# Attention on one core: the states of two heads multiplied as dense 64x64 blocks on quarters of the array

## The chip, the core and the metric

The kernel runs on one core of a Trainium2 chip. The metric is the device time of one execution in microseconds, lower is better. TensorE multiplies matrices into PSUM, which has eight banks of 2 KB in each of 128 partitions; VectorE (DVE), ScalarE (ACT) and GpSimd (POOL) do elementwise work, and DMA queues are fed by SyncE (SP) and GpSimd.

## The reference

```python
B, H, S, D = 8, 8, 576, 64          # q, k, v: batch, heads, sequence, head size
scores = q @ k.T / sqrt(D)
gamma = 1 - 2 ** (-5 - h)           # one decay for each head h
ret = scores * (gamma ** (i - j) if i >= j else 0)
attn = ret @ v                       # retention: no softmax
x = attn as (B*S, H*D) = (4608, 512)
x = moe1(x)    # cosine routing to one of 8 experts, 512 -> 1024 -> 512, relu, times the gate
x = moe2(x)    # greedy routing with a capacity of 576 tokens an expert, same sizes
```

Only the first part, attention, is touched by the change. With decay by distance, the part of a row's output that comes from earlier tiles can be written as q times a state of 64x64 for each head, the sum of gamma ** (-j) * k_j times v_j over earlier rows j, with gamma ** i put into q.

## The kernel before

The 4608 rows are 36 tiles of 128, nine tiles to two sequences of 576 rows: tile i = 0 to 3 lies in the first sequence, tile 4 holds the last 64 rows of the first and the first 64 of the second, tiles 5 to 8 lie in the second. So tile 0 of each nine has no state before it, tile 4 has one for 64 of its columns, and the other seven for all 128. Everything is float32. q and k arrive transposed, as tiles of 128 partitions (64 dimensions of the even head, then 64 of the odd one) x 4 head pairs x 128 rows; v and k also arrive by rows.

The order of the instructions is written out by hand: each engine runs them in the order of the program. The loop over T in the function moe_kernel does in iteration T, in this order: the loads of tile T + 3 (load_tile, on SP's queue, four buffers each); s_qk(T + 1); s_sel(T - 2); s_pv(T); a step of the routing of an earlier group of tiles (pump, route); s_state(T); s_kd(T + 2) on GpSimd; s_out(T - 1); s_qs(T + 2) on VectorE. The pieces are:

- s_qk, line 402: scores of the tile's diagonal block, for each head pair hp and each head e of the pair one product with 64 rows of the array, into the tiles s0 and s1, one PSUM bank each. VectorE multiplies them by the decay (line 405) into sm.
- s_sel, line 473: a small product that puts the router's logits together. Its input part is copied by ScalarE in line 461.
- s_pv: the output of the tile, transposed, in one PSUM bank o. First, where there is a state, line 416: for each head pair one product of 128x128, in which bd holds the states of the two heads as two 64x64 blocks on the diagonal, with zeros beside them; qs is q times its decay. Then line 420: for each head the product of v and sm, on 64 columns of the array, added on top. ScalarE copies o to xT (line 423).
- s_state, line 438: adds the tile's product of kd (k times its decay, made by GpSimd in line 379) and v to the state, which stays in one PSUM bank st over four tiles; ScalarE copies the two diagonal blocks to bd (line 444), in two instructions of 64x256. The zeros beside the blocks are written once, at the start (line 337), by a memset on VectorE and one on GpSimd.
- s_out: the product of xT with the expert embedding (line 458, on 32 columns of the array for each pair) and four transposes of xT (line 464) into tp, which has two buffers of one bank; ScalarE copies tp to xg (line 465).

PSUM is full: s0, s1, o, st, two banks for logits, two for tp. The routed rows are scattered to DRAM by GpSimd (line 534), group by group. In the last tiles the loads of the first expert's rows and weights begin on SP's queue (lines 311 and 241), the weights from T = 31 on, and from T = 32 on ScalarE and GpSimd or VectorE split each weight into a high and a low part (lines 267 and 272). Then come two expert stages, to which the change does nothing.

Of the kernel before, what the change touches and what calls it, by code (L numbers as in the profile page):

```python
# [9 lines left out]
F32 = mybir.dt.float32  # L10
# [3 lines left out]
AF = mybir.ActivationFunctionType  # L14
# [5 lines left out]
B, H, S, D = 8, 8, 576, 64  # L20
N, DM, E, FF = 4608, 512, 8, 1024
NT = N // 128
# [16 lines left out]
LOG2E = 1.4426950408889634  # L39


def constants():
    g = 1.0 - 2.0 ** (-5.0 - np.arange(H, dtype=np.float64))
    p = np.arange(128)
    rel = p[None, :] - p[:, None]
    dt = np.where(rel[:, None, :] >= 0, g[None, :, None] ** np.maximum(rel, 0)[:, None, :], 0.0) / 8.0
    s = np.arange(64, 192)
    gq, gs = np.empty((128, 4, 128)), np.empty((128, 4, 3))
    for e in range(2):
        for hp in range(4):  # L50
            gq[64 * e:64 * e + 64, hp, :] = (g[2 * hp + e] ** s / 8.0)[None]
            gs[64 * e:64 * e + 64, hp, :] = (g[2 * hp + e] ** np.array([128.0, 256.0, 384.0]))[None]
    tl = np.arange(9)[None, :, None]
    pos = 128 * tl + p[:, None, None]
    pos = np.where(pos >= S, pos - S, pos)
    gk = g[None, None, :] ** (-pos.astype(np.float64))
    sel = np.zeros((128, E))
    for q in range(4):
        for e in range(E):
            sel[32 * q + e, e] = 1.0  # L60
    tri = (p[:, None] < p[None, :]).astype(np.float64)
    f = np.float32
    blk = {}
    for nj in (32, 4, 2):
        r = np.arange(4 * nj)
        m = np.zeros((4 * nj, 4, E))
        m[r, r // nj, :] = 1.0
        blk[f"c_blk{nj}"] = m.reshape(4 * nj, 4 * E).astype(np.float32)
        blk[f"c_rep{nj}"] = (r[:, None] % nj == np.arange(nj)[None, :]).astype(np.float32)
    r = np.arange(8)  # L70
    blk["c_rz"] = np.repeat(np.stack([r % 2 == 0, r % 2 == 1], 1).astype(np.float32), 128, 1)
    s16 = np.zeros((16, E), np.float32)
    s16[np.arange(16), np.arange(16) % E] = 1.0
    return {
        **blk, "c_s16": s16,
        "c_dt": np.ascontiguousarray(dt.reshape(128, 4, 2, 128).transpose(0, 2, 1, 3)).astype(f), "c_gq": gq.astype(f), "c_gs": gs.astype(f),
        "c_gk": gk.reshape(128, 72).astype(f), "c_sel": sel.astype(f),
        "c_id": np.eye(128, dtype=f), "c_tri": tri.astype(f),
    }
# [78 lines left out]
def moe_kernel(ctx: ExitStack, tc: tile.TileContext, moe_expert_emb, moe_tau, moe_w1, moe_w2,  # L158
               moe2_w_gate, moe2_w1, moe2_w2, c, out, dbg=None, stage=9):
    nc = tc.nc  # L160
    V, A, G, P, SY = nc.vector, nc.scalar, nc.gpsimd, nc.tensor, nc.sync
# [151 lines left out]
    with tc.tile_pool(name="actab", bufs=1) as tab, \  # L313
# [17 lines left out]
        dt_t = tab.tile([128, 2, 4, 128], F32, name="dt")  # L331
        SY.dma_start(dt_t, c["c_dt"])
        load_tile(0, ("vr", "kr"))
        bd = []
        for i in range(2):
            t = tab.tile([128, 4, 128], F32, name=f"bd{i}")
            (G if i else V).memset(t, 0.0)
            bd.append(t)
        taub = tab.tile([128, 1], F32, name="taub")
        SY.dma_start(taub, ap(moe_tau, 0, [[0, 128], [1, 1]]))  # L340
        emb = tab.tile([E, DM], F32, name="emb")
# [20 lines left out]
        st_ps = [None]  # L362
# [45 lines left out]
        def s_pv(T):  # L408
            i = T % 9
            nq = nq_of(i)  # L410
            vt, sm = TL[T]["vr"], SM.pop(T)
            op_ = ps.tile([128, 4, 128], F32, name="o")
            if nq:
                qs, bdl = QS.pop(T), BD.pop(T)
                for hp in range(4):
                    P.matmul(op_[:, hp, :nq], bdl[:, hp, :], qs[:, hp, :nq], start=(hp == 0), stop=False,
                             skip_group_check=True)
            for hp in range(4):
                for e in range(2):
                    P.matmul(op_[64 * e:64 * e + 64, hp, :], vt[:, 2 * hp + e, :], sm[:, e, hp, :],  # L420
                             start=(hp == 0 and not nq), stop=True, skip_group_check=True)
            xT = wk.tile([128, 4, 128], F32, name="xT")
            A.activation(xT, op_, AF.Copy)  # L423
            XTT[T] = xT

        def s_state(T):
            i = T % 9
            t = TL.pop(T)
            if i == 8:
                return  # L430
            vt = t["vr"]
            r0 = 64 if i == 4 else 0
            kd = KDT.pop(T)
            if i in (0, 4):
                st_ps[0] = ps.tile([128, 4, 128], F32, name="st")
            for hp in range(4):
                for e in range(2):
                    P.matmul(st_ps[0][64 * e:64 * e + 64, hp, 64 * e:64 * e + 64], kd[r0:, 2 * hp + e, :],  # L438
                             vt[r0:, 2 * hp + e, :], start=(i in (0, 4) and hp == 0), stop=(i in (3, 7)),
                             skip_group_check=True)  # L440
            nb = bd[i % 2]
            for e in range(2):
                z = slice(64 * e, 64 * e + 64)
                A.activation(nb[z, :, z], st_ps[0][z, :, z], AF.Copy)
            BD[T + 1] = nb

        def s_out(T):
# [11 lines left out]
                         skip_group_check=True)  # L459
            part = wk.tile([128, 128], F32, name="part")  # L460
            A.activation(part, lp[:, :128], AF.Copy)
            xp = ps.tile([128, 4, 128], F32, name="tp", bufs=2)
            for hp in range(4):
                P.transpose(xp[:, hp, :], xT[:, hp, :], ident)
            A.activation(xg[:, i, :DM], xp.rearrange("p a n -> p (a n)"), AF.Copy)  # L465
# [1107 lines left out]
```

## Time and profile before

| | |
|---|---|
| runs, us | 1294.56, 1291.51, 1298.22 (median 1294.56) |
| profiled execution, us | 1298.07, of which the span is 1296.3 |
| TensorE busy | 1217.5 us (94%), 9031 matmul instructions |
| VectorE busy | 713.8 us (55%) |
| ScalarE busy | 576.9 us (45%) |
| GpSimd busy | 328.8 us (25%) |
| mean granted clock of TensorE | 0.963 of full speed |
| moved by DMA | 224.65 MB, mean 173 GB/s |

The attention stage is the first 215 us of the span or so. "Busy" is the union of the instructions' times on an engine; matmuls are pipelined and their ends are modelled, so the distance from the start of one group to the start of the next tells more than their durations. In the rows further below each line of code is named with L, PE is TensorE, PEld its weight loads, SP SyncE; "x16" is a count of instructions, and what stands in square brackets is the idle time ahead of an instruction and what ended it.

### The profile page before, as it was taken

Reading aid. Unit: us, or ns where it says so; the run is one execution under the profiler, and the core shown is the slowest. Engines: PE = TensorE matmul, PEld = TensorE weight load, DVE = VectorE, ACT = ScalarE, POOL = GpSimd, SP = SyncE. Lnnn points to the kernel's source line nnn. Section 1 sums busy time; section 2 is a strip of 40 time slices with the busy share of each in tenths; the row PEclk is TensorE's granted clock in tenths of the full one; section 3 lists DMA queues with packets and bytes.
Section 4 is the critical chain, followed back from the end, with each engine's and each line's share of the span. In section 5 each row is a group of like instructions: output and inputs, shape, how many; then the busy total and the mean of one; then the engine's idle time right before and its main releaser. Section 6 shows DMA issues by size and latency. Waiting matters only on the chain. (4 is left out here: it accounts for less than half of the span.)

```text
span 1296.3 us, 23772 instructions
## 1 busy us (share of the span) xinstructions
PE 1217.5 (94%) x9031; PEld 1043.9 (81%) x9031; DVE 713.8 (55%) x2330; ACT 576.9 (45%) x1090; POOL 328.8 (25%) x451
## 2 busy tenths in 40 slices
PE   6999976799999999999999969999999999899997
PEld 5888865789898989898887658686868878798896
DVE  4566643866565657576565756575857757021120
ACT  3566643345354535453532044353443535274550
POOL 3253454511121313030100021313133231422211
PEclk8999986899999999999999969999999999899999
DMA  7888854566767768686841244757673756677840
GB/s 261 274 282 283 268 212 147 190 164 177 195 177 183 185 168 206 163 213 159 214 127 42 90 127 119 195 137 189 143 183 85 187 152 155 184 172 182 205 100 37
DMA packets 91742, 224.65 MB, mean 173 GB/s; under 512 B 13671, under 2 KB 14447, under 8 KB 91488
## 3 DMA queue, kind: packets, MB, share of 16 engines
q0 software_dynamic: 28272, 90.35, 32.6%
q1 hardware_dynamic: 63344, 132.67, 30.7%
q8 instruction: 73, 1.20, 0.4%
q14 instruction: 53, 0.43, 0.1%
HBM read 130.26 MB, written 40.28 MB: 132 GB/s over the span
## 5 line engine op out<-in xcount | busy, mean ns | idle before, releaser
L1171 DVE SCALAR_TENSOR_TENSOR jk<-yr,wgb 128x512 bf16<-128x512 f32 x168 | 115.4, 687 | 2.4
L1250 ACT ACTIVATE hh<-l 128x320 fp32r<-128x320 f32 x128 | 55.3, 432 | 124.6 <-PE l L1249 112.3
L1333 ACT ACTIVATE yr<-l,gts 128x512 f32<-128x512 f32 x40 | 27.5, 688 | 168.9 <-PE l L1321 65.5
L251 POOL DMA_DIRECT2D w_0l<-raw x29 | 26.7, 920 | 292.2 <-ACT w_0l L248 261.8
L1436 DVE SCALAR_TENSOR_TENSOR h2l<-l,h2h 128x288 fp32r<-128x288 f32 (+2 forms) x128 | 58.3, 456 | 76.9 <-ACT h2h L1434 76.3
L1251 DVE SCALAR_TENSOR_TENSOR hl<-l,hh 128x320 fp32r<-128x320 f32 x128 | 62.4, 487 | 68.7 <-ACT hh L1250 66.2
L1434 ACT ACTIVATE h2h<-l 128x288 fp32r<-128x288 f32 (+2 forms) x128 | 52.3, 409 | 93.2 <-PE l L1454 92.2
L1461 ACT ACTIVATE o<-l 128x512 f32<-128x512 f32 (+1 forms) x40 | 23.7, 593 | 134.1 <-PE l L1493 83.8
L405 DVE TENSOR_TENSOR sm<-s,dt 128x512 f32<-128x512 f32 (+1 forms) x80 | 48.1, 633 | 57.2 <-PE s L402 44.9
L1468 POOL DMA_INDIRECT out_dram<-o,tid x40 | 42.2, 1056 | 137.9 <-ACT o L1461 90.3
L1379 POOL DMA_INDIRECT xg<-ybuf,idx x40 | 42.8, 1069 | 94.5 <-SPq L1347 58.6
L402 PE MATMUL s<-qT,kT 64*128 64x128 f32 x576 | 45.2, 298 | 11.1 <-DMA qT<-qT 8.6
L717 DVE TENSOR_TENSOR xl<-tp,xh 128x512 fp32r<-128x512 f32 (+1 forms) x41 | 27.6, 676 | 50.7 <-ACT xh L716 36.3
L931 DVE TENSOR_TENSOR cmp<-v,kb 128x1280 bf16<-128x1280 f32 (+1 forms) x42 | 54.4, 1295 | 0.2
L1464 DVE TENSOR_TENSOR o<-o,l 64x512 f32<-64x512 f32 x8 | 5.5, 690 | 86.8 <-ACT o L1461 86.8
L1247 PE MATMUL l<-xh,w_0h 128*128 128x320 f32 x128 | 41.4, 323 | 11.9 <-DVE hl L1251 7.6
L402 PEld LDWEIGHTS s<-qT,kT 64*128 64x128 f32 x576 | 38.0, 198 | 17.1 <-issue 9.4
L251 POOL DMA_DIRECT2D w_3l<-raw x29 | 25.3, 874 | 98.5 <-ACT w_3l L248 70.4
L379 POOL TENSOR_TENSOR kd<-kr,gk 128x512 f32<-128x512 f32 (+1 forms) x32 | 34.5, 1080 | 61.8 <-PE st L438 29.3
L251 POOL DMA_DIRECT2D w_2l<-raw x29 | 24.7, 851 | 97.8 <-ACT w_2l L248 61.7
L534 POOL DMA_INDIRECT xs<-xg,r_sli x36 | 37.0, 1027 | 47.0 <-ACT xg L465 26.3
L423 ACT ACTIVATE xT<-o 128x512 f32<-128x512 f32 x36 | 21.5, 597 | 59.9 <-PE o L420 56.8
(374 smaller groups left out, 4131.2 us busy)
## 6 DMA issues: line engine op xcount, KB each, us to landing
raw<-in_moe_w_dram SPq DMA_DIRECT2D x128, 512.0 KB
w_0l<-raw POOLq DMA_DIRECT2D x29, 512.0 KB
w_1l<-raw POOLq DMA_DIRECT2D x29, 512.0 KB
w_2l<-raw POOLq DMA_DIRECT2D x29, 512.0 KB
w_3l<-raw POOLq DMA_DIRECT2D x29, 512.0 KB
ybuf<-yr SPq DMA_DIRECT2D x40, 257.0 KB
xt<-xs SPq DMA_DIRECT2D x39, 261.0 KB
kT<-kT SPq DMA_DIRECT2D x36, 256.0 KB
```

The lines of the kernel that those rows point to most:

```text
L251: G.dma_start(lo, RAW[wpos[1]], accum_op=OP.add)
L402: P.matmul(sp[e][:, hp, :], kT[r, hp, :], qT[r, hp, :], start=True, stop=True, skip_group_check=True)
L405: V.tensor_tensor(sm[z, e, :, z], sp[e][z, :, z], dt_t[z, e, :, z], op=OP.mult)
L931: V.tensor_tensor(cmp, bc(v, ALLC, nj), kb.bitcast(F32)[:, None, :].to_broadcast([128, NSL, nj]), op=OP.is_ge)
L1171: V.scalar_tensor_tensor(jk, yr[:, :DM], 1.0, wgb[:, j, :], op0=OP.mult, op1=OP.mult, accum_out=L2V[:, cc, j:j + 1])
L1247: P.matmul(pp, wh[:, fz], xh[:, kk, z], start=(kk == 0), stop=False)
L1250: A.activation(hh[:, f, z], pp, AF.Relu)
L1251: V.scalar_tensor_tensor(hl[:, f, z], pp, 0.0, hh.bitcast(F32)[:, f, z], op0=OP.max, op1=OP.subtract)
L1379: G.indirect_dma_start(out=xg[:m, t, :], out_offset=None, in_=ybuf, in_offset=bass.IndirectOffsetOnAxis(ap=idx[:m, t:t + 1], axis=0))
L1434: A.activation(h2h[:, f, z], pq, AF.Relu)
L1436: V.scalar_tensor_tensor(h2l[:, f, z], pq, 0.0, h2h.bitcast(F32)[:, f, z], op0=OP.max, op1=OP.subtract)
L1468: st = G.indirect_dma_start(out=out, out_offset=bass.IndirectOffsetOnAxis(ap=TID[p][:m, t:t + 1], axis=0), in_=o[:m], in_offset=None)
```

## The change

The state of a head pair is kept as two dense 64x64 blocks, one above the other, instead of a 128x128 block with zeros: bd has half its size, needs no memset, and is copied from PSUM in one instruction of 128x256. Each 128x128 product of line 416 becomes two products of 64x64, one for each head. In every second head pair the two heads are laid the other way round in the partitions of q, k, the decay tables and the state (the function head), while the output keeps its places: so the four 64x64 products of two neighbouring pairs use four different quarters of the array. The output o takes two PSUM banks, one for the even and one for the odd pairs; tp gives up its second buffer. The products of line 420 keep their shape and number, but write to the two banks and, in every second pair, take the two column halves in the other order. ScalarE reads o with another access pattern.

```diff
--- before.py
+++ after.py
@@ -39,6 +39,10 @@
 LOG2E = 1.4426950408889634
 
 
+def head(e, hp):
+    return 2 * hp + (e ^ (hp & 1))
+
+
 def constants():
     g = 1.0 - 2.0 ** (-5.0 - np.arange(H, dtype=np.float64))
     p = np.arange(128)
@@ -48,8 +52,8 @@
     gq, gs = np.empty((128, 4, 128)), np.empty((128, 4, 3))
     for e in range(2):
         for hp in range(4):
-            gq[64 * e:64 * e + 64, hp, :] = (g[2 * hp + e] ** s / 8.0)[None]
-            gs[64 * e:64 * e + 64, hp, :] = (g[2 * hp + e] ** np.array([128.0, 256.0, 384.0]))[None]
+            gq[64 * e:64 * e + 64, hp, :] = (g[head(e, hp)] ** s / 8.0)[None]
+            gs[64 * e:64 * e + 64, hp, :] = (g[head(e, hp)] ** np.array([128.0, 256.0, 384.0]))[None]
     tl = np.arange(9)[None, :, None]
     pos = 128 * tl + p[:, None, None]
     pos = np.where(pos >= S, pos - S, pos)
@@ -73,7 +77,7 @@
     s16[np.arange(16), np.arange(16) % E] = 1.0
     return {
         **blk, "c_s16": s16,
-        "c_dt": np.ascontiguousarray(dt.reshape(128, 4, 2, 128).transpose(0, 2, 1, 3)).astype(f), "c_gq": gq.astype(f), "c_gs": gs.astype(f),
+        "c_dt": np.stack([np.stack([dt[:, head(e, hp)] for hp in range(4)], 1) for e in range(2)], 1).astype(f), "c_gq": gq.astype(f), "c_gs": gs.astype(f),
         "c_gk": gk.reshape(128, 72).astype(f), "c_sel": sel.astype(f),
         "c_id": np.eye(128, dtype=f), "c_tri": tri.astype(f),
     }
@@ -331,11 +335,7 @@
         dt_t = tab.tile([128, 2, 4, 128], F32, name="dt")
         SY.dma_start(dt_t, c["c_dt"])
         load_tile(0, ("vr", "kr"))
-        bd = []
-        for i in range(2):
-            t = tab.tile([128, 4, 128], F32, name=f"bd{i}")
-            (G if i else V).memset(t, 0.0)
-            bd.append(t)
+        bd = [tab.tile([128, 4, 64], F32, name=f"bd{i}") for i in range(2)]
         taub = tab.tile([128, 1], F32, name="taub")
         SY.dma_start(taub, ap(moe_tau, 0, [[0, 128], [1, 1]]))
         emb = tab.tile([E, DM], F32, name="emb")
@@ -409,18 +409,25 @@
             i = T % 9
             nq = nq_of(i)
             vt, sm = TL[T]["vr"], SM.pop(T)
-            op_ = ps.tile([128, 4, 128], F32, name="o")
+            op_ = ps.tile([128, 2, 512], F32, name="o")
+
+            def o(e, hp, n):
+                c0 = 64 * (e ^ (hp & 1))
+                return op_[c0:c0 + 64, hp & 1, 128 * (hp >> 1):128 * (hp >> 1) + n]
             if nq:
                 qs, bdl = QS.pop(T), BD.pop(T)
                 for hp in range(4):
-                    P.matmul(op_[:, hp, :nq], bdl[:, hp, :], qs[:, hp, :nq], start=(hp == 0), stop=False,
-                             skip_group_check=True)
+                    for e in range(2):
+                        r = slice(64 * e, 64 * e + 64)
+                        P.matmul(o(e, hp, nq), bdl[r, hp, :], qs[r, hp, :nq], start=(hp < 2), stop=False,
+                                 skip_group_check=True)
             for hp in range(4):
                 for e in range(2):
-                    P.matmul(op_[64 * e:64 * e + 64, hp, :], vt[:, 2 * hp + e, :], sm[:, e, hp, :],
-                             start=(hp == 0 and not nq), stop=True, skip_group_check=True)
+                    P.matmul(o(e, hp, 128), vt[:, head(e, hp), :], sm[:, e, hp, :],
+                             start=(hp < 2 and not nq), stop=True, skip_group_check=True)
             xT = wk.tile([128, 4, 128], F32, name="xT")
-            A.activation(xT, op_, AF.Copy)
+            A.activation(xT.rearrange("p (j s) n -> p s j n", s=2),
+                         op_[:, :, :256].rearrange("p s (j n) -> p s j n", j=2), AF.Copy)
             XTT[T] = xT
 
         def s_state(T):
@@ -432,16 +439,14 @@
             r0 = 64 if i == 4 else 0
             kd = KDT.pop(T)
             if i in (0, 4):
-                st_ps[0] = ps.tile([128, 4, 128], F32, name="st")
+                st_ps[0] = ps.tile([128, 4, 128], F32, name="st")[:, :, :64]
             for hp in range(4):
                 for e in range(2):
-                    P.matmul(st_ps[0][64 * e:64 * e + 64, hp, 64 * e:64 * e + 64], kd[r0:, 2 * hp + e, :],
-                             vt[r0:, 2 * hp + e, :], start=(i in (0, 4) and hp == 0), stop=(i in (3, 7)),
+                    P.matmul(st_ps[0][64 * e:64 * e + 64, hp, :], kd[r0:, head(e, hp), :],
+                             vt[r0:, head(e, hp), :], start=(i in (0, 4) and hp == 0), stop=(i in (3, 7)),
                              skip_group_check=True)
             nb = bd[i % 2]
-            for e in range(2):
-                z = slice(64 * e, 64 * e + 64)
-                A.activation(nb[z, :, z], st_ps[0][z, :, z], AF.Copy)
+            A.activation(nb, st_ps[0], AF.Copy)
             BD[T + 1] = nb
 
         def s_out(T):
@@ -459,7 +464,7 @@
                          skip_group_check=True)
             part = wk.tile([128, 128], F32, name="part")
             A.activation(part, lp[:, :128], AF.Copy)
-            xp = ps.tile([128, 4, 128], F32, name="tp", bufs=2)
+            xp = ps.tile([128, 4, 128], F32, name="tp")
             for hp in range(4):
                 P.transpose(xp[:, hp, :], xT[:, hp, :], ident)
             A.activation(xg[:, i, :DM], xp.rearrange("p a n -> p (a n)"), AF.Copy)
@@ -1557,7 +1562,8 @@
     q, k, v = (np.asarray(inputs[n]) for n in ("q", "k", "v"))
     laid = {nm: np.ascontiguousarray(a.transpose(0, 2, 1, 3)).reshape(N, DM) for nm, a in (("kr", k), ("vr", v))}
     for nm, a in (("kT", k), ("qT", q)):
-        t = a.transpose(1, 3, 0, 2).reshape(4, 2, D, NT, 128)
+        t = a.transpose(1, 3, 0, 2).reshape(4, 2, D, NT, 128).copy()
+        t[1::2] = t[1::2, ::-1].copy()
         laid[nm] = np.ascontiguousarray(t.transpose(3, 1, 2, 0, 4)).reshape(NT, 128, 4, 128)
     laid["w_gate_t"] = np.ascontiguousarray(np.asarray(inputs["moe2_w_gate"]).T)
     for name, a in laid.items():
```

## Rows read from the trace of the kernel before

**Rows 1.** Windows by stage: length; busy time and instructions by engine; granted clock; DMA share; GB/s.

```profile
26.00:156.00 130.00, 129.49 (x1852) 109.94 (x1853) 76.88 (x207) 80.74 (x214) 47.52 (x65) 1.00 0.84 274
...
182.00:215.00 33.00, 20.87 (x197) 17.04 (x197) 10.38 (x54) 15.62 (x37) 20.56 (x28) 0.71 0.30 114
```

**Rows 2.** Timeline of TensorE, tiles 17 to 19: start, duration, engine, line, operation.

```profile
100.52 1.09 PE L420 MATMUL o<-sm,vr 128*64 128x128 f32 x16
101.54 0.43 PE L458 MATMUL lg<-xT,enT 128*32 128x128 f32 x8
...
103.57 0.39 PE L473 MATMUL lg<-sel,part 128*128 128x8 f32 x2
103.89 1.09 PE L420 MATMUL o<-sm,vr 128*64 128x128 f32 x16
...
106.63 1.16 PE L402 MATMUL s<-qT,kT 64*128 64x128 f32 x16
107.73 0.39 PE L473 MATMUL lg<-sel,part 128*128 128x8 f32 x2
107.97 1.14 PE L416 MATMUL o<-qs,bd 128*128 128x128 f32 x8
109.04 1.09 PE L420 MATMUL o<-sm,vr 128*64 128x128 f32 x16
109.96 0.63 PE L438 MATMUL st<-vr,kd 128*64 128x64 f32 x16
110.53 0.43 PE L458 MATMUL lg<-xT,enT 128*32 128x128 f32 x8
110.88 0.65 PE L464 MATMUL tp<-ident,xT 128*128 128x128 f32 x4
111.47 0.71 PE L402 MATMUL s<-qT,kT 64*128 64x128 f32 x8
```

**Rows 3.** Windows of 10 ns on line 458 alone: how many instructions are in flight.

```profile
110.55:110.56 0.01, 0.01 (x4) 1.00 0.06 0
...
110.68:110.69 0.01, 0.01 (x8) 1.00 1.01 418
```

**Rows 4.** Timeline of TensorE and GpSimd, tile 31.

```profile
165.24 0.39 PE L473 MATMUL lg<-sel,part 128*128 128x8 f32 x2
...
166.50 1.09 PE L420 MATMUL o<-sm,vr 128*64 128x128 f32 x16
...
167.24 1.03 POOL L379 TENSOR_TENSOR kd<-kr,gk 64x512 f32<-64x512 f32 x1 [6.08 <-DMA xs<-xg,r_sli]
...
168.33 0.68 PE L438 MATMUL st<-vr,kd 64*64 64x64 f32 x16 [0.74 <-POOL kd L379]
168.94 0.43 PE L458 MATMUL lg<-xT,enT 128*32 128x128 f32 x8
```

**Rows 5.** Groups by line and shape, TensorE, 0 to 207 us: count, busy, mean ns, idle.

```profile
L416 PE MATMUL o<-qs,bd 128*128 128x128 f32 x224 | 33.7, 296 | 0.0
...
L416 PE MATMUL o<-qs,bd 128*128 128x64 f32 x32 | 4.3, 278 | 0.0
```

**Rows 6.** Groups by line and shape, ScalarE, 26 to 156 us.

```profile
L444 ACT ACTIVATE bd<-st 64x256 f32<-64x256 f32 x48 | 18.0, 374 | 3.1 <-PE lg L458 1.1 <-PE tp L464 1.0 <-PE st L438 0.7
```

**Rows 7.** Timeline, tile 1.

```profile
19.79 2.07 PE L416 MATMUL o<-qs,bd 128*128 128x128 f32 x8
```

**Rows 8.** Timeline of ScalarE and TensorE, tiles 32 to 35.

```profile
179.34 1.06 ACT L267 ACTIVATE w_0h<-raw 128x1024 fp32r<-128x1024 f32 x1 [7.80 <-DMA raw<-in_moe_w_dram]
...
182.04 0.60 PE L473 MATMUL lg<-sel,part 128*128 128x8 f32 x2 [5.40 <-ACT part L461]
...
182.49 2.05 PE L416 MATMUL o<-qs,bd 128*128 128x128 f32 x8
...
198.44 0.58 ACT L423 ACTIVATE xT<-o 128x512 f32<-128x512 f32 x1
```

**Rows 9.** Windows of 4 us, all engines.

```profile
52.00:56.00 4.00, 4.00 (x66) 3.43 (x65) 1.90 (x13) 2.20 (x6) 0.00 (x0) 1.00 1.04 371
```

## The prediction

> **What bounds the kernel now.** I read the windows by stage first. From 26 to 156 us of the span TensorE is busy 129.49 of 130.00 us at a granted clock of 1.00, while VectorE has 76.88, ScalarE 80.74 and GpSimd 47.52; the DMA engines are at 0.84 of their time and 274 GB/s [rows 1]. The change sits in this attention stage, and nothing in the diff touches the two expert stages behind it. A busy TensorE isn't yet one at its limit, so I read next one tile in order of time: line 402 starts at 106.63 and again at 111.47, and between them lines 473, 416, 420, 438, 458 and 464 follow each other with no idle time in any row [rows 2]. So a tile takes 4.84 us, and a shorter group on TensorE is a shorter tile, as long as no other chain of work is as long. The time to look at is from the start of one group to the start of the next, not the durations, which overlap.
>
> **The changed product.** Now, from the start of line 473 (two instructions, 128x128 array) to the start of line 420 pass 1.31 us (107.73 to 109.04), of which the first 0.24 lie before line 416, whose eight instructions use the whole array one by one [rows 2]. After the change the same work is 16 instructions (four pairs, two heads, and every f32 product is two instructions, as line 420 with its 8 products and x16 shows), each on a quarter of the array.
>
> How many run at once decides everything, and no row shows quarters on four corners with 128 columns. The nearest is line 458: four products on four column strips, eight instructions. At 110.55 four are in flight, at 110.68 all eight [rows 3]: the four strips start together, then the four second halves. Line 402 does the same with two row halves (16 instructions in 106.63 to 107.73). I call such a step a round. Line 420 has 16 instructions on two halves, eight rounds, and takes 1.02 us where another shape of tile follows (100.52 to 101.54); line 458 has two rounds and takes 0.35 (110.53 to 110.88) [rows 2]. So a round is (1.02 - 0.35) / 6 = 0.11 us. Four corners at once are four rounds, 0.35 + 2 x 0.11 = 0.57. In return the shape of the tile now changes behind line 473 as well: where line 420 follows it directly, in the tile that has no state, 0.32 pass instead of 0.24 (103.57 to 103.89) [rows 2]. New: 0.32 + 0.57 = 0.89, against 1.31: 0.42 us less a tile. The bounds: four bare rounds are 0.44, which saves 0.55; two corners at a time are eight rounds, 0.32 + 0.35 + 6 x 0.11 = 1.33, which saves nothing; one at a time sixteen rounds, 0.32 + 0.35 + 14 x 0.11 = 2.21, which loses 0.90. I take 0.42, as line 458 is the nearest row.
>
> The instructions with 64 columns: today 1.26 us (165.24 to 166.50) from line 473 on, hardly less than with 128. The nearest row is line 438 in the same tile, 64x64 tiles with 64 columns: eight rounds in 0.61 (168.33 to 168.94) [rows 4]. Half of that is 0.31; the change of shape at its end isn't halved, so I take 0.37 (between 0.31 and 0.61). New 0.69, saved 0.57 (0.33 to 0.63).
>
> How many tiles: line 416 has 224 instructions with 128 columns and 32 with 64 [rows 5], eight to a tile: 28 full tiles and 4 half ones; four tiles of 36 have no state.
>
> **The other edits.** The products of sm and vr keep their number and their tile shape, but write to two banks, and the heads of every second pair swap halves, so that two products in a row now go to the same half of the array columns. If instructions wait only for their own half, as line 458 suggests, each half still has eight rounds: no cost. If not, it is the slower rival below. The evacuation of the state becomes one instruction of 128x256 for two of 64x256, each 374 ns [rows 6]: ScalarE gets some 0.4 us back a tile. It has 80.74 busy of 130 us [rows 1], so in the steady part this is worth nothing, nor would xT's strided reading cost anything, were it 0.1 us longer; it moves the tail (below). The transposes of xT lose their second buffer: those of a tile must now wait until the previous tile's xg is copied, which lies a whole tile earlier except at the end (tile 34 behind tile 33, under 1 us late). Behind the waiting transposes TensorE has the last products, whose output ScalarE reads only at 198.44 [rows 8], so I put it at nothing; without that cover it is 0.9. The two memsets at the start lie beside the first loads: nothing, 0.5 at most. Loads, their sizes and their order on SP's queue stay as they are, as do the scatters on POOL's.
>
> **From tiles to the end.** Up to tile 28 the saving runs through: 21 full tiles at 0.42 are 8.8, three half ones (4, 13, 22) at 0.57 are 1.7. Tile 1 runs before the clock has risen: its eight instructions take 2.07 us [rows 7] where those of [rows 2] take 1.14 from the first start to the last end, so 0.42 x 1.8 = 0.8. Sum 11.3.
>
> What tiles 29 to 32 save I count as lost. Tile 31's state products already wait 0.74 us for kd, and GpSimd can start kd only at 167.24, after 6.08 us idle for a scatter to land [rows 4]. That scatter is started from the routing of tile 28, so the chain behind it doesn't shorten: the wait grows by what tiles 29, 30 and 31 save, 0.42 + 0.42 + 0.57, to 2.1 us. Next in line behind it ScalarE stands 7.80 us for the first expert weights, up to 179.34, and line 473 of TensorE stands 5.40 behind that, up to 182.04 [rows 8]; tile 32's 0.42 goes into this wait. If the chain did shorten, 1.8 more would come.
>
> In the tail tile 33 runs at the low clock (2.05 us for its eight instructions [rows 8], so 0.8 saved); one state copy less ahead of part is 0.4 on ScalarE, for which line 473 waits there; tile 34 brings 0.4. What tile 35 saves on TensorE is lost, as ScalarE comes to its output only at 198.44, behind a row of copies of which one is gone: 0.4. Together 2.0.
>
> One stretch can't go faster: while the zero rows are written, around 52 to 56 us, the DMA engines are at 1.04 and 371 GB/s [rows 9]. I take off two tiles there, 0.8. The sum: 11.3 + 2.0 - 0.8 = 12.5 us.
>
> The profiled execution took 1298.07 us, a span of 1296.3 and 1.8 around it; 12.5 less is 1285.6. It lies 3.5 above the median of the runs, 1294.56, so the median after comes to 1282.
>
> **The rivals.** *Two corners at a time.* A quarter could wait for its row or its column neighbour. For it: no row has both halves of rows and of columns busy at once. Against: four column strips do overlap, and so do two row halves, into two banks on the same partitions (line 402 into its two tiles s). Then a full tile costs 1.33 for 1.31, a half one 0.32 + 0.61 for 1.26; over 24 tiles that is no change within 1 us, and the two ScalarE terms remain: 1294.
>
> *DMA takes it back.* A tile in 4.42 instead of 4.84 us asks for 274 x 4.84 / 4.42 = 300 GB/s at a share of 0.92. For it: slices at 1.04 exist already, and scatters take up to 6 us to land as it is. Against: 371 GB/s have been reached [rows 9]. If only half of the 11.3 were kept: 1288.
>
> *Slower: strict order.* If an instruction started only after all earlier ones had started, the second half of a product would hold up the next product's first half. The new product would need nine rounds, 0.32 + 0.35 + 7 x 0.11 = 1.44 for 1.31, and the products of sm and vr, with up to four instructions in a row on one half, some 12 rounds instead of 8, +0.44. That is +0.57 a tile; over some 28 tiles +16: 1310. It decides from the point where the products of sm and vr take 1.4 us or more. Against it stand the four instructions in flight at 110.55 [rows 3]: in strict order, with halves side by side, it would be two at most. How the halves of different products lie in the queue no row shows.
>
> The Trainium skill has this rule: "TensorE: Matmul & The Clock Gate", section "The mechanism" of the part on packing small matmuls, says that matmuls start and end in program order and that only weight loads are pulled ahead. By that rule the sum would be this rival's; the trace speaks against it, as far as the four in flight can, and I leave it a small chance.
>
> **How the numbers follow.** The forecast, four corners at once: 0.74. Two corners: 0.09. DMA: 0.11. Strict order, or another loss of its kind: 0.06. The forecast's own range is 1277 (bare rounds and the lost 1.8 come in) to 1288 (bounds of the half tiles, more given back, and the runs' own scatter, which was 1291.5 to 1298.2). To leave out no more than 2 in 10 the range goes to 1295, which takes in two corners and DMA. A measurement can tell some 0.5%, 6.5 us. Faster by more than that: nine tenths of the forecast's case and a part of DMA's, 0.71. Within: the rest of these and most of two corners, 0.20. Slower: 0.09.
>
> **What would show it.** In the profile after, the product of qs and bd should read x16 with 64x64 tiles, start 0.32 behind the start of line 473's product and have the next group 0.57 behind its own start, with four in flight at its first instants; line 402's starts should lie 4.42 apart; the products of sm and vr should still take 0.92 to 1.02; the state copy should be one row of about 0.37; the wait before tile 31's state products should be near 2 us, the 5.4 us wait near tile 33 still there, and the attention stage some 12 us shorter with the stages behind it as long as before. A product of 1.0 us or more, or tiles that stay at 4.8, would make the prediction wrong; so would stages behind it that move by more than a few us.

## The result, and the profile after

The changed kernel takes 1281.45 us, the median of 7 runs (1277.17 to 1288.07), and the kernel before 1294.56 beside it (7 runs). The ratio is 0.9905, with a 95% interval of 0.9879 to 0.9931: 13.1 us or 1% less. The forecast was 1282 us, 12.5 us less. The profiled execution took 1281.45 us, its span 1279.7.

The stage first, as in [rows 1]. The columns are the length, busy time and instructions of TensorE, its weight loads, VectorE, ScalarE and GpSimd, then granted clock, DMA share and GB/s.

```profile
26.00:144.00 118.00, 117.06 (x1980) 95.97 (x1980) 73.60 (x197) 70.22 (x183) 46.51 (x64) 0.99 0.88 289
```

TensorE is as full as before, and no other engine has come near it. The DMA engines rose from 0.84 to 0.88 and from 274 to 289 GB/s: the same bytes in less time.

One tile in order of time, to be laid beside [rows 2] (start, duration, engine, line, operation):

```profile
110.47 1.16 PE L402 MATMUL s<-qT,kT 64*128 64x128 f32 x16
111.57 0.39 PE L478 MATMUL lg<-sel,part 128*128 128x8 f32 x2
111.89 0.67 PE L422 MATMUL o<-qs,bd 64*64 64x128 f32 x16
112.48 1.09 PE L426 MATMUL o<-sm,vr 128*64 128x128 f32 x16
113.41 0.64 PE L445 MATMUL st<-vr,kd 128*64 128x64 f32 x16
113.97 0.43 PE L463 MATMUL lg<-xT,enT 128*32 128x128 f32 x8
114.33 0.66 PE L469 MATMUL tp<-ident,xT 128*128 128x128 f32 x4
114.91 0.60 PE L402 MATMUL s<-qT,kT 64*128 64x128 f32 x6
```

The tile takes 4.44 us (110.47 to 114.91) where it took 4.84. From line 478 (473 before) to the products of sm and vr pass 0.91 us instead of 1.31; every other step has kept its length within 0.02 us. Four instructions start together, in the first 20 ns of that row (a window on line 422 alone; its columns as in [rows 3]):

```profile
111.89:111.91 0.02, 0.02 (x4) 1.00 0.79 307
```

The tail, which answers to [rows 4] and [rows 8] (TensorE and GpSimd):

```profile
159.87 1.04 POOL L379 TENSOR_TENSOR kd<-kr,gk 64x512 f32<-64x512 f32 x1 [6.61 <-DMA xs<-xg,r_sli]
...
160.97 1.12 PE L445 MATMUL st<-vr,kd 64*64 64x64 f32 x16 [2.18 <-POOL kd L379]
...
163.64 2.08 PE L402 MATMUL s<-qT,kT 64*128 64x128 f32 x16
...
173.00 0.39 PE L478 MATMUL lg<-sel,part 128*128 128x8 f32 x2 [1.42 <-ACT part L466]
...
204.68 0.60 PE L1252 MATMUL l<-xh,w_0h 128*128 128x320 f32 x1 [4.53 <-DVEq L738]
```

The wait for kd has grown from 0.74 to 2.18 us. Behind it line 402 takes 2.08 us for 1.16, and the wait for part is 1.42 instead of 5.40. The clock shows why line 402 is slow (windows of TensorE's wait and of the time after it; the last three columns are clock, DMA share and GB/s):

```profile
158.50:161.00 2.50, 0.32 (x8) 0.08 (x4) 1.40 (x5) 0.60 (x1) 1.07 (x2) 0.88 0.10 34
161.00:165.50 4.50, 4.50 (x44) 3.59 (x44) 0.00 (x0) 1.87 (x5) 3.09 (x4) 0.50 0.17 61
```

After it had been busy for 0.32 of 2.50 us, TensorE was granted 0.50 of its clock, that is 1.2 of 2.4 GHz, for the next 4.5 us.

The first product of the experts starts at 204.68 us, 10.25 before the kernel before's (214.93). The expert stages behind it took 1075.0 us where the first profile of before had 1081.4. In twelve further profiles, of kernels of both forms, they took 1067.6 to 1076.1. So the profiled execution of before was a long one (3.5 us above its median). The second profiles of the two kernels, shown further below, have 1067.6 and 1068.1 us there, so the 6.4 us are not counted for the change.

### The profile page after: what moved, and what is told of

It reads as the page before. It is cut to its first block, busy times and chain, and to the rows that moved or that the text cites. A ratio compares the mean times of both kernels' runs of the same rounds, so it can differ in the third digit from the quotient of the medians.

```text
span 1279.7 us, 24248 instructions
## 1 busy us (share of the span) xinstructions
PE 1200.2 (94%) x9287; PEld 1024.6 (80%) x9287; DVE 715.4 (56%) x2329; ACT 566.3 (44%) x1058; POOL 326.8 (26%) x450
## 5 line engine op out<-in xcount | busy, mean ns | idle before, releaser
L1216 DVE SCALAR_TENSOR_TENSOR jk<-wz,wgb 128x512 bf16<-128x512 f32 x64 | 45.9, 717 | 1.0
```

The lines of the kernel that those rows point to most:

```text
L1216: V.scalar_tensor_tensor(jk, wz, 1.0, wgb[:, j, :], op0=OP.mult, op1=OP.mult, accum_out=M7[:, i, j:j + 1])
```

## The experiments

The kernel before took 1294.6 us (median) beside the change; 1292.8 beside two_corners, rows_in_turn, halves_in_turn and no_product; 1291.7 beside kd_weights_routing_xt; and 1281.4 beside the other seven. So kernels are compared by their ratio to the before that ran beside them. "First expert product" is its start in the profile; it stands at 214.93 and 209.59 in the two profiles of before.

| kernel | median us | ratio (95%) | first expert product |
|---|---|---|---|
| change | 1281.45 | 0.9905 (0.9879 to 0.9931) | 204.68 |
| after_again (the change once more) | 1268.32 | 0.9901 (0.9871 to 0.9931) | 198.07 |
| two_corners | 1287.4 | 0.9958 (0.9938 to 0.9979) | 209.78 |
| two_corners_again | 1277.12 | 0.9965 (0.9939 to 0.9990) | 208.96 |
| rows_in_turn | 1279.49 | 0.9900 (0.9867 to 0.9932) | 201.37 |
| halves_in_turn | 1289.05 | 0.9974 (0.9950 to 0.9997) | 211.22 |
| no_product (results differ; 2 runs) | 1267.34 | 0.9805 (0.9760 to 0.9851) | 192.12 |
| before_again | 1280.54 | 0.9994 (0.9973 to 1.0015) | 209.59 |
| kd_all_rows | 1267.01 | 0.9891 (0.9857 to 0.9925) | 197.88 |
| kd_all_rows_again | 1267.48 | 0.9897 (0.9867 to 0.9928) | 195.01 |
| kd_all_rows_early_weights | 1263.06 | 0.9855 (0.9824 to 0.9885) | 195.76 |
| kd_weights_routing | 1265.39 | 0.9859 (0.9822 to 0.9896) | 193.63 |
| kd_weights_routing_xt | 1275.55 | 0.9891 (0.9851 to 0.9932) | 192.82 |

**Are the four corners what pays?** (two_corners, two_corners_again)

```diff
 def head(e, hp):
-    return 2 * hp + (e ^ (hp & 1))
+    return 2 * hp + e
...
-                c0 = 64 * (e ^ (hp & 1))
+                c0 = 64 * e
...
-        t[1::2] = t[1::2, ::-1].copy()
```

> Every pair laid the same way, so that the dense states meet qs only on two opposite quarters of the array (rows 0 to 63 with columns 0 to 63, rows 64 to 127 with columns 64 to 127); the dense state, its one copy, the two banks and the single tp buffer stay. If the four corners at once are what pays, the 16 instructions need eight rounds instead of four: 0.32 + 0.35 + 6 x 0.11 = 1.33 from the start of the product of part to that of the products of sm and vr, for 0.92 measured after the change; +0.41 over 24 full tiles and about +0.25 over four half ones, 11 us, so 1292 us. If it is the smaller state, the single copy or the two banks that pay, the time stays at 1281 to 1284.

> The kernel with two corners once more. It was 0.9958 of the time of before (0.9938 to 0.9979), 5.4 us less, where its tiles (4.86 us, four half ones of 4.60 for 4.93) account for some 0.5 to 1.5 us up to tile 31. If the 5.4 are the runs' scatter, it now comes out at 0.997 to 1.000; if something outside the tiles pays with every form of the change (the smaller state, its single copy, one tp buffer), it comes out at 0.995 to 0.997 again, and the corners are worth only the difference to the changed kernel, some 0.5%.

The timeline of the second run, and two windows on line 422 alone:

```profile
110.49 0.39 PE L478 MATMUL lg<-sel,part 128*128 128x8 f32 x2
110.80 1.09 PE L422 MATMUL o<-qs,bd 64*64 64x128 f32 x16
111.83 1.09 PE L426 MATMUL o<-sm,vr 128*64 128x128 f32 x16
```
```profile
110.80:110.82 0.02, 0.02 (x2) 1.00 0.58 205
```

Two in flight instead of four, 1.34 us from line 478 to line 426 instead of 0.91, tiles of 4.87: as priced. On the same chip within one series, the first expert product of two_corners_again comes at 208.96 and that of after_again at 198.07: the four corners are worth 10.9 us in the attention stage by these marks, and 8 by the ratios (0.9965 less 0.9901), give or take some 5 by their intervals.

The rest is not explained. Both runs stay below before, by 5.4 and 4.5 us, and their intervals leave out less than 1.3. Their marks are 0.6 us before to 0.2 behind the second profile of before (209.59), and 5 to 6 before the first (214.93), whose execution was a long one. The expert stages took 1071.9 and 1072.0 us in the two profiles, which is inside the scatter. The profiled execution of the first lies 3.9 us below its median and that of the second 5.7 above, so profiles that differ by this much can't show where 4 us lie. Where these 4 to 5 us lie, if they are more than before's own scatter, stays open.

**Does an instruction wait for its place in the queue?** (halves_in_turn, rows_in_turn)

```diff
-            for hp in range(4):
-                for e in range(2):
+            for c0 in range(2):
+                for hp in range(4):
+                    e = c0 ^ (hp & 1)
                     P.matmul(o(e, hp, 128), vt[:, head(e, hp), :], sm[:, e, hp, :],
```

> The changed kernel with the products of sm and vr put in the queue by halves of the array columns: first all four heads that go to columns 0 to 63 (eight instructions), then the four for columns 64 to 127. Nothing else differs. If an instruction waits only for its own half of the array, however far ahead in the queue the other half's work stands, the group still takes 0.92 us and the time stays at 1281 (within 4). If instructions start in the order of the queue, the group takes sixteen rounds, 0.35 + 14 x 0.11 = 1.89, +0.97 over 36 tiles: 1313 to 1316. A value between says that TensorE looks ahead by a few instructions only.

Neither came. Lines 427 and 446 are here the products of sm and vr and those of the state:

```profile
108.41 1.25 PE L427 MATMUL o<-sm,vr 128*64 128x128 f32 x13
109.39 0.27 PE L446 MATMUL st<-vr,kd 128*64 128x64 f32 x1
109.50 0.27 PE L427 MATMUL o<-sm,vr 128*64 128x128 f32 x1
...
109.72 0.73 PE L446 MATMUL st<-vr,kd 128*64 128x64 f32 x13
110.38 0.43 PE L464 MATMUL lg<-xT,enT 128*32 128x128 f32 x8
```

Products of the state start before products of sm and vr that stand ahead of them in the queue: TensorE starts matmuls out of order where they go to different parts of the array. The two groups together take 1.97 us (108.41 to 110.38) for 1.49 after the change (112.48 to 113.97), and with 0.48 us a tile the first expert product comes 9.85 us later than with rows_in_turn, which ran beside it. Sixteen rounds would have cost twice that. Two windows of 10 ns on line 427 alone show where the other half of the columns comes in:

```profile
108.85:108.86 0.01, 0.01 (x2) 1.00 1.16 410
108.92:108.93 0.01, 0.01 (x4) 1.00 0.00 0
```

Up to 108.9 one half runs alone: five of its instructions start, a first step of 0.16 us and three of 0.11 apart, and two are in flight, as a record is 0.27 us long and the next starts before it ends. Then both halves run. At that point three of the first half's eight instructions have yet to start.

```diff
-                for hp in range(4):
-                    for e in range(2):
+                for e in range(2):
+                    for hp in range(4):
                         r = slice(64 * e, 64 * e + 64)
```

> The changed kernel with the quarter products put in the queue by halves of the rows: first the four heads on rows 0 to 63 (eight instructions, corners alternating between the two column halves), then the four on rows 64 to 127. Nothing else differs. If each corner goes on by itself, the group keeps its four rounds, 0.60 us, and the time stays at 1281 (within 4). If TensorE can't look eight instructions ahead, two corners run after the other two, up to eight rounds, 1.03 us: +0.44 over 24 tiles and +0.2 over four, 11 us, so 1292.

```profile
105.71 0.68 PE L422 MATMUL o<-qs,bd 64*64 64x128 f32 x16
106.32 1.09 PE L426 MATMUL o<-sm,vr 128*64 128x128 f32 x16
```

```profile
105.72:105.73 0.01, 0.01 (x2) 1.00 0.00 0
105.74:105.76 0.02, 0.02 (x4) 1.00 0.53 205
```

The group takes 0.61 us for 0.59 (the two windows are on line 422 alone). The corners on rows 64 to 127 start some 20 ns after the others, past the other six of the eight instructions that stand ahead of them in the queue, three for each of two corners. Both runs fit one picture: a part of the array takes one running instruction and three waiting ones, and a fifth holds up the queue. No run varies that number, so it stays a reading. The Trainium skill, "TensorE: Matmul & The Clock Gate", section "The mechanism", says that matmuls start and end in program order; these rows disagree.

**What bounds the stage next?** (no_product)

```diff
-                for hp in range(4):
-                    for e in range(2):
-                        r = slice(64 * e, 64 * e + 64)
-                        P.matmul(o(e, hp, nq), bdl[r, hp, :], qs[r, hp, :nq], start=(hp < 2), stop=False,
-                                 skip_group_check=True)
```

> The products of qs and bd are left out altogether, so that a tile does not see the states of the tiles before it; the routing of the tokens differs with that, so only the attention stage is read. What bounds the stage next? If TensorE still does: from the start of the product of part to that of sm and vr 0.32 instead of 0.92, tiles of 3.84 instead of 4.44 us, by tile 28 some 21 x 0.60 + 3 x 0.39 = 13.8 us less, DMA at 289 x 4.44 / 3.84 = 334 GB/s. If DMA bounds it (share 0.88 now, by the same ratio 1.02): TensorE waits for kT, qT, kr or vr in many tiles, and less than half of the 13.8 us comes.

A window over its stage, and its timeline at tile 22, a half tile:

```profile
26.00:96.00 70.00, 69.91 (x1102) 58.38 (x1100) 47.33 (x129) 46.90 (x124) 31.97 (x43) 1.00 0.97 333
```
```profile
92.59 1.16 PE L402 MATMUL s<-qT,kT 64*128 64x128 f32 x16
...
96.44 1.26 PE L402 MATMUL s<-qT,kT 64*128 64x128 f32 x16
...
105.82 1.06 PE L440 MATMUL st<-vr,kd 64*64 64x64 f32 x16 [2.94 <-POOL kd L379]
```

Tiles of 3.85 us with TensorE busy 69.91 of 70 us, at 333 GB/s: the DMA engines don't bound the stage even there. What is late next is kd of the half tiles: 2.94 us at tile 22, at half the clock behind it. Line 402 of tile 22 comes 16.2 us earlier than with rows_in_turn beside it (108.75 there), that of tile 28 9.8, and the first expert product 9.25.

**Where do the tail's microseconds go?** (kd_all_rows, kd_all_rows_again)

```diff
-                G.tensor_tensor(kd[r0:], TL[T]["kr"][r0:], gk_t[r0:, i, :, None].to_broadcast([128 - r0, H, D]),
+                G.tensor_tensor(kd, TL[T]["kr"], gk_t[:, i, :, None].to_broadcast([128, H, D]),
```

> The changed kernel, with kd computed on all 128 rows in the four half tiles too (the other 64 rows are not read). In the trace after, kd of tile 31, on 64 rows, stands 6.61 us on GpSimd until the earlier scatters have landed, and TensorE stands 2.18 behind it; whole-row kd of other tiles shows no such wait. Theory A: that wait lies in the chain of the first expert weights too, since the fifth scatter of its group is queued behind kd on GpSimd, the loads of xt behind that scatter's landing, and the raw weights behind xt on SP's queue. Then scatter, xt, weights and TensorE all come some 5 us earlier, tile 32 keeps the full clock, and the time is about 1276. Theory B, the prediction's: what is gained ahead of the weights is lost in waiting for them; the wait of 2.18 goes, that of 1.42 near tile 33 grows by as much, and the time moves by less than 1.5 us: 1280 to 1281.

> kd on all 128 rows, now on the same chip as the changed kernel. The first time it was 0.9891 of before, where the changed kernel was 0.9905 on another chip. Theory A (the wait of kd lies in the chain of the first weights) expects 4 to 5 us less than the changed kernel run beside it, a ratio of 0.986 to 0.987; theory B (what is gained is lost in the wait for the weights) expects at most 1.5 us less, 0.989 to 0.990.

The chain in after_again, which ran beside kd_all_rows_again, and then the same four rows of the latter (kd of tile 31, the fifth scatter, w_0h, the first expert product):

```profile
153.38 1.46 POOL L379 TENSOR_TENSOR kd<-kr,gk 64x512 f32<-64x512 f32 x1 [5.75 <-DMA xs<-xg,r_sli]
155.14 0.99 POOL L539 DMA_INDIRECT xs<-xg,r_sli  x1 [0.16 <-POOL spacer L538]
164.26 1.06 ACT L271 ACTIVATE w_0h<-raw 128x1024 fp32r<-128x1024 f32 x1 [5.23 <-DMA raw<-in_moe_w_dram]
198.07 0.60 PE L1252 MATMUL l<-xh,w_0h 128*128 128x320 f32 x1 [4.43 <-PEq L738]
```
```profile
148.53 1.05 POOL L379 TENSOR_TENSOR kd<-kr,gk 128x512 f32<-128x512 f32 x1
149.78 1.23 POOL L539 DMA_INDIRECT xs<-xg,r_sli  x1 [0.18 <-issue]
161.07 1.06 ACT L271 ACTIVATE w_0h<-raw 128x1024 fp32r<-128x1024 f32 x1 [4.55 <-DMA raw<-in_moe_w_dram]
195.01 0.61 PE L1252 MATMUL l<-xh,w_0h 128*128 128x320 f32 x1 [4.61 <-DVEq L738]
```

The mechanism is theory A's. On 64 rows kd waits for the scatters, on 128 it doesn't. The wait is in the program as it was built: the trace has five semaphore instructions of line 379 ahead of the 64-row kd, the last at 153.2 us, and one ahead of the 128-row kd. The fifth scatter comes 5.4 us earlier, xt (154.87 for 158.08), weights and experts some 3 us. But the 4 to 5 us of theory A did not come: of these 3 us the medians show 0.8 (1267.48 for 1268.32), the ratio of 0.9897 lies in the range of theory B, and ratios of this width can't tell 0.8 from 3. Whether it pays stays open.

> The changed kernel, unchanged, beside three others on one chip. Its ratio to the kernel before was 0.9905 (0.9879 to 0.9931); by the tiles it should be 0.990 to 0.991 on any chip, with tiles of 4.44 us and a wait of some 2 us before the state products of tile 31. The idle time inside the state products of five tiles (0.37 to 0.71 us each, with nothing that releases it) was there in its first profile and in the one with the quarter products by rows, and in none of the two with kd on all rows, which ran on another chip: if the chip made it, it goes or stays with the chip and is the same in this run as in that with kd on all rows; if the wait of kd made it, it is here and not there.

The wait was there (2.18 us again). The idle time inside the state products is in the first profile, with its gap of 0.39 us, as here in those of tile 25 (the last four of 16 instructions):

```profile
132.78 0.35 PE L445 MATMUL st<-vr,kd 128*64 128x64 f32 x4 [0.39 <-issue]
```

It is in rows_in_turn too, gone in after_again and in both runs with kd on all rows, and back once in the last kernel below, where before took 1291.7. So it goes with the runs in which before itself took 1292 to 1295 us, not with kd, and not with the chip: rows_in_turn and after_again ran on the same one. What makes it is open.

> The kernel before, unchanged, for a second profile of it. Its first profile was of an execution of 1298.1 us, 3.5 above the median. If the 5 us by which the kernel with two corners beat the kernel before, with tiles no shorter, lie in the start and the tail of the profiled execution, a second profile at about 1293 us shows tiles of 4.84 us again, but tile 2 starting some 1 us earlier, and a wait for the first weights of 2 to 4 us in place of 5.4, with the first product of the experts at 211 to 213 us instead of 214.9. If not, they come from the copy of the state or the half tiles, and the second profile has the same marks as the first.

The second profile of before, and then that of after_again, on another chip, beside which before took the same 1281.4 us (line 402 of tiles 4 and 28):

```profile
29.04 1.16 PE L402 MATMUL s<-qT,kT 64*128 64x128 f32 x16
...
142.90 1.16 PE L402 MATMUL s<-qT,kT 64*128 64x128 f32 x16
...
178.79 0.47 PE L473 MATMUL lg<-sel,part 128*128 128x8 f32 x2 [4.64 <-ACT part L461]
...
209.59 0.60 PE L1247 MATMUL l<-xh,w_0h 128*128 128x320 f32 x1 [4.48 <-DVEq L733]
```
```profile
27.65 1.16 PE L402 MATMUL s<-qT,kT 64*128 64x128 f32 x16
...
132.35 1.16 PE L402 MATMUL s<-qT,kT 64*128 64x128 f32 x16
```

The wait for the first weights is 4.64 us here and not 2 to 4, but the first expert product comes 5.3 us earlier than in the first profile of before, of which the start up to tile 4 makes 1.7 and the tail behind tile 28 2.75. So these marks move by several us with nothing changed, and this pair, whose executions lie 1.5 and 0.3 us below their medians, is the better one to compare. It is still one execution of each kernel.

**Can the tail be shortened further?** (three kernels on top of kd_all_rows; each keeps the edits of the one before it)

```diff
-WL, LX, GE = (31,5,4)
+WL, LX, GE = (30,5,4)
```

> As the kernel with kd on all rows, and the first four weight loads put on SP's queue one tile earlier (after tile 30 instead of 31), ahead of the loads of xt, which wait for scatters to land. If the wait of TensorE near tile 33 and the wait of ScalarE before w_0h (5.71 us after) come from the place of the weights in that queue, both go, and the time is 2 to 4 us below that of the kernel with kd on all rows alone. If the 2 MB of weights only push the tiles' own loads back (DMA share 0.88), TensorE waits for kT or qT of tiles 33 to 35 instead, and nothing is gained or up to 3 us lost.

```diff
-TP = 32; WC={31:0,32:0,33:0,34:0,99:1}
+TP = 33; WC={31:0,32:0,33:0,34:0,99:1}
```

> kd on all rows, the first weights one tile earlier, and the third step of the routing of tiles 25 to 29 one tile later (TP 33 for 32). With the first two alone (0.9855 of before) TensorE's state products of tile 32 are followed by 1.81 us of waiting for r_cum, behind which the clock falls for tile 33 (line 402 takes 2.00 us for 1.09). If that wait is what is late next, it goes, the clock stays, and 3 to 4 us more come: 0.982 to 0.983. If the routing is needed that early, since its scatters end last before the experts' first product, the wait only moves to the end and the ratio stays at 0.985 to 0.987.

```diff
-WL, LX, GE = (30,5,4)
+WL, LX, GE = (30,5,5)
```

> As the kernel with kd on all rows, early weights and later routing, and the early loads of xt made after the sixth group of scatters instead of the fifth (GE 5 for 4), so that on SP's queue they stand behind the loads of the last tile and not ahead of them. In the kernel without this edit SP's queue stands until 158.75 us for scatters to land, tile 35's kT and qT are asked for at 160.15, and TensorE waits 1.31 us for qT before tile 35's line 402. If that is all, the wait goes and 1 to 1.5 us come: 0.985 of before. If xt is needed earlier than it then lands, the first product of the experts comes later by as much as the scatters of the sixth group are later, some 5 us, and the ratio is 0.988 to 0.990.

Each took away the wait that it aimed at, and another came. With early weights w_0h waits for nothing, but the routing of tiles 25 to 29 does:

```profile
162.28 0.18 PE L521 MATMUL lg<-r_cum,onesb 128*128 128x40 bf16 x1 [1.81 <-DVE r_cum L510]
```

With TP at 33 that wait is gone and qT of tile 35 is late by 1.31 us; with xt behind the last tile's loads, that is gone, and the single tp buffer is late:

```profile
172.67 1.12 PE L469 MATMUL tp<-ident,xT 128*128 128x128 f32 x4 [3.37 <-ACT xg L470]
```

The first expert product moves by 2 and then 1 us (195.76, 193.63, 192.82). By their ratios, 0.9855 and 0.9859, the first two of these three kernels are, beside no_product, which leaves work out, the fastest that were run, and faster than before without doubt; their intervals overlap with that of the changed kernel (0.9879 to 0.9931). The third, at 0.9891, gained nothing that its runs show.

## Why the prediction was right, point by point

- **Four corners at once**: right. Four in flight in the first 20 ns, 0.32 and 0.59 us for 0.32 and 0.57. Half tiles go from 1.26 to 0.72 (line 478 at 116.00, line 426 at 116.72 in the first profile), forecast 0.69. The products of sm and vr kept 0.92 to 0.93. A tile is 4.44 for 4.42 forecast.
- **Sum to tile 28, 11.3**: 10.55 in the better pair (142.90 less 132.35), at tile 28's line 402, where its own 0.42 is still to come, so that 10.9 are due. Up to tile 4's line 402 it is 1.39, forecast 0.8 + 0.42 = 1.22 (tiles 1 and 2); from there to tile 28, 9.16, forecast 19 x 0.42 + 3 x 0.57 = 9.7. In the first pair it was 7.5: the start gave 0.04, as tile 3's line 402 still ran at half the clock (2.04 us from 25.40), and idle time without a releaser in five tiles took some 2.
- **The 0.8 off for the DMA engines**: not needed. TensorE waits for no load in that stretch, nor at 333 GB/s.
- **Tiles 29 to 32 lost**: right in kind. The wait for kd became 2.18 us, forecast 2.1. But the wait of 5.40 for the first weights did not stay near tile 33: it is 1.42, and none in after_again. The clock took a part of its place, which the prediction had not seen: behind the longer wait for kd it halves, and tile 32 takes 6.78 us from one line 402 to the next (163.64 to 170.42), for 5.59 before. The rest came back as a longer wait behind the last tile (next point).
- **The tail, 2.0**: this is the term that was mis-sized. In the better pair 1.0 is left (66.69 less 65.72 us from tile 28's line 402 to the first expert product) of 2.0 and tile 28's 0.42; in the first pair, whose before had the long wait, 2.7. The prediction went by TensorE's and ScalarE's work there. The end of the path is another, VectorE behind GpSimd, in the routing of tiles 30 to 33 (before_again, then after_again):

```profile
191.52 2.35 POOL L272 TENSOR_TENSOR w_3l<-raw,w_3h 128x1024 fp32r<-128x1024 f32 x1
193.24 0.69 DVE L495 TENSOR_TENSOR r_eq<-lgs,r_mx 128x32 f32<-128x32 f32 x1
194.66 0.19 PE L515 MATMUL lg<-r_oh,tri 128*128 128x32 bf16 x1 [2.53 <-DVE r_cum L503]
```
```profile
179.99 2.34 POOL L276 TENSOR_TENSOR w_3l<-raw,w_3h 128x1024 fp32r<-128x1024 f32 x1
178.79 3.60 DVE L500 TENSOR_TENSOR r_eq<-lgs,r_mx 128x32 f32<-128x32 f32 x1
183.12 0.21 PE L520 MATMUL lg<-r_oh,tri 128*128 128x32 bf16 x1 [5.38 <-DVE r_cum L508]
```

  r_eq starts 14.45 us earlier after the change but ends 11.54 earlier, both times 0.06 us behind GpSimd's w_3l. In all fourteen profiles it ends 0.05 to 0.06 us behind w_3l, however late it starts, and the first expert product comes 15.5 to 16.0 us behind w_3l. GpSimd's work from w_0l to the end of w_3l takes as long as before, 16.7 and 16.9 us, so what TensorE and ScalarE save behind the landing of the weights is waited away. In the first pair it is 18.9 and 16.9, as w_3l of before waits 2.28 us for ScalarE's w_3h there.
- **The state copy**: one row of 0.38 us; 0.37 forecast. **The single tp buffer**: nothing for the changed kernel that counts (0.33 to 0.64 us of wait at tile 34, with the tail's other waits beside it), up to 3.37 once the waits ahead of it are gone.
- **The stages behind unmoved**: 1067.6 and 1068.1 us in the better pair.
- **The rivals**: DMA is out by no_product. Strict order is out by halves_in_turn and by the four in flight. Two corners is out for the change itself. Its price, 0.8 us less than before, fits the marks beside before_again, and is some 4 us too small by the ratios.

So the sum came out at 11.5 in the attention stage of the better pair, forecast 12.5. The medians differ by 13.1, but the interval of the ratio runs from 8.9 to 15.7 us, so the 1.6 between may be scatter. That the forecast came so near is in part luck: the tail brought 1.4 us too little, and the 0.8 taken off for the DMA engines, which weren't lost, made up for more than half of that. And by the ratios the corners are 0.5 to 0.6% of the 1%; the other 4 to 5 us that the two-corner runs show are, but for 0.8, in no term of the sum.

## What to carry to other kernels

Where a product has zero blocks, count rounds and not columns: on quarters of the array four small f32 products run in the time of one, provided that the heads are laid so that all four corners are in use (here corners with the same columns also write to different banks; one bank was not tried). The order in the queue may differ from that by a few instructions for each part of the array, but not by eight on the same one. A tile that gets shorter moves the whole stage only until the next transfer or scatter that does not: look for it before the sum is made, and count the clock that falls behind its wait. Look also at which engine ends last behind it: in the tail here it was GpSimd, which had nothing to do with the change.

## What the runs showed of the hardware that was not expected

- TensorE starts matmuls out of the queue's order across parts of the array, as above, even those of another group of the same tile shape.
- Behind a product that GpSimd has begun, r_eq and r_cum on VectorE don't just run slower: they end when that product does. r_eq in the routing of tiles 30 to 33 takes 0.66 to 3.60 us in the fourteen profiles and ends each time 0.05 to 0.06 us behind w_3l; in after_again it starts within w_2l and stands through w_3l too. On the five tiles of an earlier group, with no product of GpSimd beside it, it takes 0.20. Five additions of r_cum take 0.95 us with nothing beside them and 3.88 in kd_weights_routing, where one of them ends 0.02 us behind w_0l and another 0.02 behind kd.

  The Trainium skill, "GPSIMD Engine Reference", section "Specifications", has VectorE and GpSimd share their way to SBUF for instructions with two SBUF inputs, as all of these are; the rows agree.
